# The last expert's second product in seven half-size products, in an attention and mixture-of-experts kernel

## The chip, the cores and the metric

The kernel runs on one core of a Trainium2 chip. The metric is the device time of one execution in microseconds (us). TensorE (PE in the profile) does the matrix products, VectorE (DVE) and ScalarE (ACT) the elementwise work, GpSimd (POOL) issues the gathers and scatters of token rows, SyncE (SP) issues the other transfers.

## The reference

An attention over a window of keys and over block summaries gives 3072 rows of 512 numbers. They go through a mixture of 8 experts, of which each row uses two:

```
logits = x @ w_gate;  noisy = logits + log1p(exp(x @ w_noise)) * noise
top2 = the two largest of noisy;  top2_w = softmax over these two
for e in range(8):
    for k in range(2):
        mask = top2[:, k] == e
        h = maximum(x[mask] @ w1[e], 0)              # 512 -> 1024
        out[mask] += top2_w[mask, k, None] * (h @ w2[e])   # 1024 -> 512
```

All data are 32-bit floats.

## The kernel before

After the attention the experts run one after the other, with room for 768 to 832 tokens each. Every 32-bit operand is split into two 16-bit floats, a high part and a rest (hi and lo), and every product is done in three passes: hi by hi, hi by lo, lo by hi. A split costs one copy on ACT (hi) and one subtraction on DVE (lo).

From the third expert on, the first product (x by w1) is done in seven products of half-size blocks instead of eight. The function `seven(e, i, u)` does product u = 1 to 7 for quarter i of the hidden features: `prod` issues its matmuls (L1365), and the sums that the scheme wants are built up in PSUM, with a copy on ACT (L1386, L1389) and an addition on DVE (L1391, L1393). The four blocks of hidden activations leave through a relu on ACT to `HT[0]` (hi, L1397) and a subtraction on DVE to `HT[1]` (lo, L1400).

The second product (h by w2) is plain: `mm2_part` issues for each chunk of 128 tokens 24 matmuls of 512 columns (8 row blocks of w2, three passes, L1437) into a PSUM buffer `pt`; `mm2_out` multiplies the chunk by the gate weight and adds the row that an earlier expert left (DVE, L932), and `y_scatter` writes it to `out` (POOL, L90). The earlier rows come by `prev_gather` (POOL, L90). The last expert (e = 7) has 768 tokens: six chunks.

The order of the work on each engine is the order in which the program is written. What is done for the next expert, or ahead of a use, is hung into that order by a table: `on(t, f, ...)` puts a call at step t, and `hook(t)` issues what stands there. A step of expert e thus holds loads (`w_load`, SP, L736), splits (`w_hi` on ACT, L741; `w_lo` on DVE, L759) and gathers. Four staging buffers (`stage`) take the loads. `og` is one PSUM tile of two banks, `b2` and `b5` are lists of two banks each, and `G["b1", i]` is `og[:, 0]` or a `pt` buffer in turn.

Of the kernel before, what the change touches and what calls it, by code (L numbers as in the profile page):

```python
# [8 lines left out]
F32 = mybir.dt.float32  # L9
# [4 lines left out]
AF = mybir.ActivationFunctionType  # L14
OP = mybir.AluOpType
# [5 lines left out]
P = 128  # L21
# [3 lines left out]
DM = H * D  # L25
E, F = 8, 1024
# [10 lines left out]
H0 = 384  # L37
# [7 lines left out]
SW = 16 * (D + 1)  # L45
# [5 lines left out]
GN = 4  # L51
WS = 16384.0
GROUP0 = 3
XS, W1S, W2S = 128.0, 32.0, 1024.0
# [9 lines left out]
def attn_moe(ctx, tc, qt, kt, vt, wgn, noise, w1, w2, out):  # L64
    nc = tc.nc
# [4 lines left out]
    psum = ctx.enter_context(tc.tile_pool(name="psum", bufs=1, space=PSUM))  # L70
# [4 lines left out]
    stage = ctx.enter_context(tc.tile_pool(name="stage", bufs=4))  # L75
# [3 lines left out]
    work = ctx.enter_context(tc.tile_pool(name="work", bufs=2, side="right"))  # L79
# [134 lines left out]
    late = []  # L214
# [212 lines left out]
    G = {}  # L427
# [290 lines left out]
    WT = {}  # L718
# [5 lines left out]
    SG, EV = {}, {}  # L724

    def w_load(e, i):
        s = stage.tile([P, SW], F32, name="stg")[:, :1024]
        SG[e, i] = s
        if i == 0:
            EV[e] = nc.values_load(eid[0:1, e:e + 1], engines=[mybir.EngineType.SP], min_val=0, max_val=E - 1) if e else 0  # L730
        if i < 4:
            nc.sync.dma_start(s, w1.rearrange("e d f -> (e d) f")[bass.ds(EV[e] * DM + i * P, P)])
        else:
            i -= 4
            rows = bass.ds(EV[e] * F + 2 * i * P, 2 * P)
            nc.sync.dma_start(s.rearrange("p (c d) -> p c d", c=2),  # L736
                              w2.rearrange("e f d -> (e f) d")[rows].rearrange("(c p) d -> p c d", p=P))
# [46 lines left out]
    def tb_of(e, c):  # L784
        return TB0[:, c] if e == 0 and c < 3 else TB[:, e, c]
# [85 lines left out]
    ow = {}  # L871
    pi_ = [0]

    def prev_gather(e, c):
        n = min(P, CAPS[e] - c * P)
        pv = PREV[pi_[0] % len(PREV)]
        pi_[0] += 1
# [12 lines left out]
        ow.setdefault(e, []).append(g)  # L890
        return pv
# [483 lines left out]
    def seven(e, i, u):  # L1375
        h = CAPS[e] // 2
        if u == 1:
            G["b1", i] = psum.tile([P, 512], F32, name="pt", bufs=2) if i % 2 else og[:, 0]
        b1, b2, b5 = G["b1", i][:, :h], G["b2"][i % 2][:, :h], G["b5"][i % 2][:, :h]
        hh, hl = HT  # L1380
        f = i + (4 if u in (4, 7) else 0)
        t = slice(0, h) if u in (2, 4) else slice(h + tail(e), 2 * h + tail(e))
        a, b = ((0, 0), (1, 1), (6, 2), (2, 6), (3, 3), (4, 5), (5, 4))[u - 1]
        prod(e, i, a, b, {1: b1, 2: b1, 3: b5, 5: b5}.get(u, b2), u in (1, 5))
        if u == 1:
            nc.scalar.activation(b2, b1, AF.Copy)  # L1386
# [12 lines left out]
        def lo():  # L1399
            nc.vector.scalar_tensor_tensor(hl[:, f, t], src, 0.0, hh[:, f, t], op0=OP.max, op1=OP.subtract)  # L1400

        return hi, lo

    def seven_head(e):
        if e == 2:
# [88 lines left out]
    for e in range(1, E):  # L1494
# [7 lines left out]
        if e == 1:  # L1502
# [9 lines left out]
        else:  # L1512
# [13 lines left out]
            if e > 2:  # L1526
                on(4, w_load, e, 6)
                on(4, w_load, e, 7)
        if n + 1 < E:
            on(40 if e == 1 else 43, xs_gather, n + 1, 0)  # L1530
            on(42 if e == 1 else 47, xs_gather, n + 1, 1)
        if n < E:
            on(44, w_load, n, 4)
            on(44, w_load, n, 5)
        if e == 1:
            on(48, w_load, n, 6)
            on(48, w_load, n, 7)
        for t in (17, 20, 23):
            on(t, prev)
        if e == 1:  # L1540
            for half in range(2):
                for f in range(FC):
# [169 lines left out]
```

## Time and profile before

| | us |
|---|---|
| median of 3 runs | 642.95 (642.61 to 643.33) |
| the profiled execution, as timed | 644.06 |
| its span in the trace | 642.2 |
| PE busy | 621.3 (97%), 5295 matmuls |
| DVE busy | 481.8 (75%) |
| ACT busy | 316.2 (49%) |
| POOL busy | 249.3 (39%) |

The trace comes from one execution. Busy time is the sum of an engine's instructions in the span. In tables of stretches a row holds the stretch and its length, then the busy time and, in brackets, the number of instructions of PE, PEld (PE's weight loads, which run beside the matmuls), DVE, ACT and POOL in this order, then the granted clock of TensorE as a share of full speed, the share of the DMA engines, and GB/s. In rows of single instructions the columns are the start, the time, the engine, the line, the operation, its output and inputs, and in square brackets how long the engine had been idle and what released it. An instruction's own time overlaps the next one's; the distance of two starts is what one costs in a row of them.

### The profile page before, as it was taken

How to read it: one execution, taken by the hardware profiler on the slowest of the kernel's cores; microseconds unless marked ns; L12 is line 12 of the kernel's file. 1: busy time of each engine (PE TensorE's matmuls, PEld its weight loads, DVE VectorE, ACT ScalarE, POOL GpSimd, SP SyncE). 2: the span in 40 equal slices, each digit the busy share in tenths (PEclk: the TensorE clock that was granted, in tenths of full speed). 3: DMA queues.
4: the chain of work that ended last, by engine and by line, in shares of the span. 5: the costliest groups of instructions: out<-in, count | busy, mean ns of one | idle time of the engine just before them, and what ended most of it. 6: DMA issues, size and time to landing. Idle time of an engine off the chain costs nothing. (4 is left out here: it accounts for less than half of the span.)

```text
span 642.2 us, 14122 instructions
## 1 busy us (share of the span) xinstructions
PE 621.3 (97%) x5295; PEld 360.3 (56%) x5295; DVE 481.8 (75%) x1039; ACT 316.2 (49%) x692; POOL 249.3 (39%) x432
## 2 busy tenths in 40 slices
PE   8899998899999999999999999999999999999995
PEld 7778787765554544555455544554554455445542
DVE  5858999789797598188868887987888679757510
ACT  4958988851163453075437534653464255425300
POOL 4443234203254434532573266336523532333041
PEclk9999999999999999999999999999999999999999
DMA  9999979778369786647986597769786768773021
GB/s 304 321 252 299 282 244 322 233 280 275 130 213 174 209 211 175 224 120 143 204 265 158 130 226 245 176 130 244 216 188 154 218 198 166 177 200 111 2 96 50
DMA packets 123707, 127.91 MB, mean 199 GB/s; under 512 B 83242, under 2 KB 86674, under 8 KB 123630
## 3 DMA queue, kind: packets, MB, share of 16 engines
q1 hardware_dynamic: 111838, 90.66, 53.6%
q0 software_dynamic: 11792, 36.27, 18.3%
q8 instruction: 43, 0.70, 0.5%
q14 instruction: 34, 0.28, 0.1%
HBM read 81.85 MB, written 25.61 MB: 167 GB/s over the span
## 5 line engine op out<-in xcount | busy, mean ns | idle before, releaser
L90 POOL DMA_INDIRECT out_dram<-y,tb x52 | 69.4, 1335 | 168.0 <-DVE y L932 129.6
L90 POOL DMA_INDIRECT xg<-xd,tb x54 | 60.4, 1119 | 119.8 <-DVE rh L1393 31.6
L1437 PEld LDWEIGHTS <-hth 128*128 128x128 f16 x576 | 56.4, 98 | 66.6
L932 DVE SCALAR_TENSOR_TENSOR y<-pt,tb,prev 128x512 f32<-128x512 f32 x42 | 31.5, 749 | 66.1 <-PE pt L1437 48.8
L1365 PEld LDWEIGHTS <-w1h 128*128 128x128 f16 x504 | 48.8, 98 | 38.8 <-issue 5.1
L1437 PE MATMUL pt<-w2h,htl 128*128 128x512 f16 x288 | 69.0, 379 | 0.0
L1437 PE MATMUL pt<-w2l,hth 128*128 128x512 f16 x288 | 69.0, 379 | 0.0
L1437 PE MATMUL pt<-w2h,hth 128*128 128x512 f16 x288 | 69.0, 379 | 0.0
L1365 PEld LDWEIGHTS <-w1l 128*128 128x128 f16 x504 | 49.3, 98 | 34.9
L90 POOL DMA_INDIRECT prev<-out_dram,tb x45 | 52.1, 1159 | 23.8 <-issue 13.4
L333 ACT ACTIVATE p<-s,nm 128x120 f32<-128x120 f32 x192 | 50.8, 376 | 0.8
L855 PE MATMUL h<-xte,w1h 128*128 128x384 f16 (+2 forms) x248 | 48.9, 336 | 0.0
L1437 PEld LDWEIGHTS <-htl 128*128 128x128 f16 x288 | 28.2, 98 | 34.0
L1354 ACT ACTIVATE w1h<-stg 128x768 f16<-128x768 f32 (+1 forms) x24 | 22.7, 944 | 40.4 <-DVE stg L1345 40.4
L1397 ACT ACTIVATE hth<-h 128x384 f16<-128x384 f32 (+4 forms) x48 | 23.8, 496 | 35.6 <-PE h L1365 34.1
L1365 PE MATMUL h<-xte,w1h 128*128 128x384 f16 (+4 forms) x180 | 39.7, 329 | 1.5 <-DVE h L1391 1.2
L1354 ACT ACTIVATE w1l<-stg 128x768 f16<-128x768 f32 (+1 forms) x24 | 22.5, 942 | 37.3 <-DVE stg L1345 37.3
L1365 PE MATMUL h<-xte,w1l 128*128 128x384 f16 (+4 forms) x180 | 39.7, 329 | 0.0
L1318 ACT ACTIVATE x<-xt 128x512 f16<-128x512 f32 (+2 forms) x44 | 26.5, 626 | 23.4 <-issue 20.1
L1345 DVE TENSOR_TENSOR stg<-stg 128x256 f32<-128x256 f32 x96 | 36.2, 418 | 0.8
L855 PEld LDWEIGHTS <-w1h 128*128 128x128 f16 x256 | 24.7, 98 | 19.4 <-issue 1.0
L1400 DVE SCALAR_TENSOR_TENSOR htl<-h,hth 128x384 f16<-128x384 f32 (+4 forms) x48 | 26.3, 562 | 11.8 <-ACT hth L1397 11.5
(310 smaller groups left out, 1296.7 us busy)
## 6 DMA issues: line engine op xcount, KB each, us to landing
stg<-in_w_dram SPq DMA_DIRECT2D x64, 512.0 KB
q<-in_qt_dram SPq DMA_DIRECT2D x24, 256.0 KB
out_dram<-xg SPq DMA_DIRECT2D x8, 768.0 KB
kb<-in_kt_dram SPq DMA_DIRECT2D x6, 768.0 KB
hth<-in_vt_dram SPq DMA_DIRECT2D x12, 260.0 KB
htl<-in_vt_dram SPq DMA_DIRECT2D x16, 195.0 KB
ve<-in_vt_dram SPq DMA_DIRECT2D x12, 260.0 KB
xd<-x SPq DMA_DIRECT2D x10, 256.0 KB
```

Source lines behind the costliest of these rows:

```text
L90: return nc.gpsimd.indirect_dma_start(**kw)
L333: nc.scalar.activation(PE_[t][:, a, hp, :], SC[t][:, a, hp, :], AF.Exp, bias=NM[t][:, 1, a, hp:hp + 1], scale=0.125)
L855: nc.tensor.matmul(ph[:, :n], w1_of(w, wn, c, f), x[:, xo + c, c0:c1], start=(k == 0), stop=(k == 11))
L932: nc.vector.scalar_tensor_tensor(y, py[:, :d], gw, pv[:, :d], op0=OP.mult, op1=OP.add)
L1318: nc.scalar.activation(t[:r, c:c + k], src, AF.Copy)
L1345: nc.vector.tensor_tensor(o, x, y, op=op)
L1354: nc.scalar.activation(hi, x, AF.Copy, scale=W1S)
L1365: nc.tensor.matmul(ph[:, :h], w[:, la, a, P * j:P * j + P], x[:, j, :h], start=start and k == 0, stop=k == 5, skip_group_check=True)
L1397: nc.scalar.activation(hh[:, f, t], src, AF.Relu)
L1400: nc.vector.scalar_tensor_tensor(hl[:, f, t], src, 0.0, hh[:, f, t], op0=OP.max, op1=OP.subtract)
L1437: nc.tensor.matmul(py, x, wv[:, f, :], start=st, stop=sp, skip_group_check=True)
```

## The change

Only the last expert (e = 7) is changed.

The second product is written as seven products of half-size blocks. The hidden activations are four blocks A11, A12, A21, A22 (384 tokens by 512 features), w2 is four blocks B11 to B22 (512 by 256). Four sums of activation blocks are made on DVE (`z_sums`), on the 32-bit values as they leave PSUM, and need A11 and A22 once more as 32-bit copies on ACT (`plus`). Four differences of weight blocks are made on DVE (`z_weight`). All sums are then split into hi and lo (`z_split`, `z_wsplit`). Each product has three chunks of 128 tokens with 12 matmuls of 256 columns, so 252 matmuls of 256 columns stand for 144 of 512. What the products share is built up in PSUM: A11·B11 is copied once (L1546), A1·B1 is copied to SBUF (`q5`, L1612) and added there (L1621). The output leaves in 18 steps of 128x256 on DVE (`put`, L1589) in place of six of 128x512.

Four more things move. The w2 of expert 7 is loaded during expert 6 into its token buffers (`G["zs"]`, the buffers of hi and lo tokens) instead of `stage`. All six gathers of earlier rows stand at steps 14 to 24 of expert 7. The chunks of a product stand in the order 0, 2, 1, with groups of PSUM banks p1, p2, p4, p5. The scatters stand at the end. The `else` below `plain` in the diff is the branch for the end of the last quarter, and the last block of the diff is in the table of steps of expert 6.

```diff
     def w_load(e, i):
-        s = stage.tile([P, SW], F32, name="stg")[:, :1024]
+        if "zs" in G and i >= 4:
+            s = G["zs"][i - 4]
+        else:
+            s = stage.tile([P, SW], F32, name="stg")[:, :1024]
...
     def seven(e, i, u):
...
+        if e == E - 1 and u in (2, 7, 3, 4):
+            return z_sums(i, u, src, hi, lo)
...
+    def z_sums(i, u, src, hi, lo):
...
+        def plus(name):
+            ZS[name, i] = work.tile([P, DM], F32, name="x", bufs=5)[:, :H0]
+            nc.scalar.activation(ZS[name, i], src, AF.Relu)
+        def hi_():
+            if u != 3:
+                hi()
+            if u in (2, 7):
+                plus({2: "a11", 7: "a22"}[u])
+        def lo_():
+            if u != 3:
+                lo()
+            if u == 3:
+                nc.vector.scalar_tensor_tensor(part(1), src, 0.0, ZS["a22", i], op0=OP.max, op1=OP.add)
+                nc.vector.scalar_tensor_tensor(part(3), src, 0.0, ZS["a11", i], op0=OP.max, op1=OP.subtract)
+                nc.vector.tensor_tensor(part(2), ZS[1, i], ZS["a11", i], op=OP.subtract)
+            elif u == 4:
+                nc.vector.scalar_tensor_tensor(part(4), src, 0.0, ZS[2, i], op0=OP.max, op1=OP.subtract)
...
+    def z_prod(a, b, ps, c, start, fs=range(4)):
+        za, zb = G["za"][a], G["zb"][b]
+        for la, lb in ((0, 0), (0, 1), (1, 0)):
+            for f in fs:
+                nc.tensor.matmul(ps[c], za[la][:, f, c * P:c * P + P], zb[lb][:, f], start=start, stop=True,
+                                 skip_group_check=True)
+                start = False
...
+    def last_expert(e):
...
+        order = (0, 2, 1)
+        p1 = [og[:, c // 2, HD * (c % 2):HD * (c % 2) + HD] for c in range(3)]
+        p2 = [x[:, :HD] for x in (b2[0], b5[1], b5[0])]
+        p5 = [x[:, :HD] for x in (og[:, 0], b2[1], og[:, 1])]
+        def plain(c):
+            z_prod("a11", "b11", p1, c, c != 1)
+            nc.scalar.activation(p2[c], p1[c], AF.Copy)
...
+            else:
+                plain(0)
+                h7[1]()
+                plain(2)
+                for j in range(2):
+                    z_wsplit(j, 1, 1)
+            h3 = seven(e, i - 1, 3)
...
+            if i == 4:
+                plain(1)
+            h4 = seven(e, i - 1, 4)
...
+        def put(c, half, ps):
+            y = ZP[c][:, HD * half:HD * half + HD]
+            nc.vector.scalar_tensor_tensor(y, ps, gws[c], y, op0=OP.mult, op1=OP.add)
+        for fs in (range(3), range(3, 4)):
+            for c in order:
+                z_prod("a12", "b21", p1, c, False, fs)
...
+        for c in order:
+            z_prod("a22", 4, p4, c, c != 1)
+        for c in order:
+            put(c, 0, p1[c])
...
+        for c in order:
+            z_prod(1, 1, p5, c, True)
+            nc.scalar.activation(q5[:, c], p5[c], AF.Copy)
...
+        for c in order:
+            z_prod(2, 2, p2, c, False)
+            nc.vector.tensor_tensor(p5[c], p2[c], q5[:, c], op=OP.add)
+        for c in order:
+            put(c + 3, 1, q5[:, c])
+        for j in (1, 2, 3):
+            z_split(4, j, 1)
+        for c in order:
+            z_prod(3, 3, p2, c, False)
+            put(c + 3, 0, p2[c])
+            put(c + 3, 1, p2[c])
+            y_scatter(e, c + 3, ZP[c + 3])
+        for c in order:
+            z_prod(4, "b22", p5, c, False)
+            put(c, 1, p5[c])
+            y_scatter(e, c, ZP[c])
...
+            if n == E - 1:
+                on(37, z_init)
+                for t, i in ((38, 4), (39, 6), (41, 5), (42, 7)):
+                    on(t, w_load, n, i)
+                for j in range(2):
+                    on(45 + j, z_weight, j, 3)
+                    on(45 + j, z_weight, j, 1)
-        if n < E:
+        if n < E - 1:
             on(44, w_load, n, 4)
             on(44, w_load, n, 5)
```

The kernel after is longer than the one before, so its lines have other numbers: L1391, L1393, L1397 and L1400 of before are L1395, L1397, L1401 and L1404 of after.

On VectorE the first place is the end of the first product of expert 7, from the addition of product 6 in the last quarter to the split of the block A22 (`h`, `rh` and `pt` are PSUM banks or the buffer of the block A22). Before:

```order
L1391 TENSOR_TENSOR h<-h,p_7895 128x384
L1400 SCALAR_TENSOR_TENSOR htl<-pt,hth 128x384
L1400 SCALAR_TENSOR_TENSOR htl<-h,hth 128x384 x2
L1393 TENSOR_TENSOR rh<-h,p_7895 128x384
L1400 SCALAR_TENSOR_TENSOR htl<-rh_3813,hth 128x384
```

On VectorE, the same place now:

```order
L1395 TENSOR_TENSOR h<-h,p_7930 128x384
L1404 SCALAR_TENSOR_TENSOR htl<-pt,hth 128x384
L1439 SCALAR_TENSOR_TENSOR xt<-h,x 128x384
L1440 SCALAR_TENSOR_TENSOR xt<-h,x 128x384
L1441 TENSOR_TENSOR xt<-xt,x 128x384
L1404 SCALAR_TENSOR_TENSOR htl<-h,hth 128x384
L1443 SCALAR_TENSOR_TENSOR xt<-h,xt 128x384
L1498 SCALAR_TENSOR_TENSOR w1l_320<-xl,w1h_319 128x1024
L1397 TENSOR_TENSOR rh_3813<-h,p_7930 128x384
L1404 SCALAR_TENSOR_TENSOR htl<-rh_3813,hth 128x384
```

Between the first addition and the one that makes `rh` there were three instructions; now there are seven: four more sums, one split less of a hidden block, and a split of 1024 weight columns.

On ScalarE, at the same place, now:

```order
L1401 ACTIVATE hth<-pt 128x384
L1427 ACTIVATE x<-pt 128x384
L1500 ACTIVATE w1h_319<-xg_165 128x512
L1500 ACTIVATE w1h_319<-xg_166 128x512
L1401 ACTIVATE hth<-h 128x384
L1401 ACTIVATE hth<-rh_3813 128x384
L1427 ACTIVATE x<-rh_3813 128x384
L1546 ACTIVATE h<-o 128x256 x3
L1401 ACTIVATE hth<-h 128x384
```

The three copies of A11·B11 (L1546) stand behind the relu and the 32-bit copy of the block that VectorE's `rh` addition makes. Before, only relus stood here.

The second place is the end of the program on VectorE, from the additions of `q5` on. Before, its last rows were six like this one, each behind a chunk of 24 matmuls, and a scatter on POOL behind each:

```order
L1400 SCALAR_TENSOR_TENSOR htl<-rh_3813,hth 128x384
L1400 SCALAR_TENSOR_TENSOR htl<-h,hth 128x384 x2
L932 SCALAR_TENSOR_TENSOR y<-pt,tb,prev_2952 128x512
L932 SCALAR_TENSOR_TENSOR y<-pt,tb,prev_2950 128x512
L932 SCALAR_TENSOR_TENSOR y<-pt,tb,prev_2951 128x512
```

On VectorE, the end now:

```order
L1621 TENSOR_TENSOR o<-h,stg 128x256 x2
L1621 TENSOR_TENSOR h<-h,stg 128x256
L1589 SCALAR_TENSOR_TENSOR y<-stg,tb,y 128x256 x3
L1472 TENSOR_TENSOR w1l_2943<-stg,w1l_2943 128x768
L1472 TENSOR_TENSOR w1l_2943<-xt,w1l_2943 128x384
L1472 TENSOR_TENSOR w1l_2943<-w1l_320,w1l_2943 128x384
L1589 SCALAR_TENSOR_TENSOR y<-h,tb,y 128x256 x6
L1589 SCALAR_TENSOR_TENSOR prev_2952<-o,tb,prev_2952 128x256
L1589 SCALAR_TENSOR_TENSOR prev_2951<-o,tb,prev_2951 128x256
L1589 SCALAR_TENSOR_TENSOR prev_2950<-h,tb,prev_2950 128x256
```

Fifteen puts and splits now lie between the last addition and the end. On POOL six scatters follow the sixfold puts without a gather between them; the six gathers stand a product earlier.

On SyncE the third place is the last part of expert 6. Before, the loads of expert 7's w2 stood behind all token transposes of expert 7 and went to `stage`:

```order
L1334 DMA_TRANSPOSE w2h_2944<-x 128x6x128
L1334 DMA_TRANSPOSE w2l_2945<-x 128x8x128
L1334 DMA_TRANSPOSE xte<-x 128x6x128
L1334 DMA_TRANSPOSE xte<-x 128x8x128
L736 ISA
L736 DMA stg<-in_w_dram 128x2x512
```

On SyncE, the same place now:

```order
L739 ISA
L739 DMA xte<-in_w_dram 128x2x512
L1338 DMA_TRANSPOSE w2h_2944<-x 128x6x128
L1338 DMA_TRANSPOSE w2l_2945<-x 128x8x128
L739 ISA
L739 DMA xte<-in_w_dram 128x2x512
L1338 DMA_TRANSPOSE xte<-x 128x6x128
L1338 DMA_TRANSPOSE xte<-x 128x8x128
```

Two of the four loads now stand between and ahead of these transposes, and their target is the buffer that held expert 6's tokens.

## Rows read from the trace of the kernel before

**Rows 1.** Table by stretch: first product, then second product, of the last expert

```profile
580.00:600.00 20.00, 20.00 (x125) 12.05 (x124) 14.40 (x23) 11.28 (x21) 5.29 (x8) 1.00 0.27 79
600.00:620.00 20.00, 20.00 (x100) 9.68 (x99) 5.36 (x10) 2.48 (x5) 4.40 (x8) 1.00 0.17 54
```

**Rows 2.** Chain of waits, its end (start, time, engine, what)

```profile
605.39 29.58 PE pt L1437 x137
...
635.00 0.76 DVE y L932
```

**Rows 3.** Instructions of PE, second product

```profile
614.08 1.89 PE L1437 MATMUL pt<-w2h,hth 128*128 128x512 f16 x8
...
619.26 1.89 PE L1437 MATMUL pt<-w2h,hth 128*128 128x512 f16 x8
```

**Rows 4.** Instructions of PE, first product, third quarter

```profile
588.12 0.81 PE L1365 MATMUL h<-w2l,w1h 128*128 128x384 f16 x4
...
589.10 0.81 PE L1365 MATMUL h<-w2l,w1l 128*128 128x384 f16 x4
```

**Rows 5.** Instructions of VectorE, first quarter into second

```profile
580.84 0.55 DVE L1391 TENSOR_TENSOR h<-h,p 128x384 f32<-128x384 f32 x1
581.30 2.35 DVE L759 SCALAR_TENSOR_TENSOR w2l<-stg,w2h 128x1024 f16<-128x1024 f32 x2
583.57 0.55 DVE L1393 TENSOR_TENSOR rh<-h,p 128x384 f32<-128x384 f32 x1
```

**Rows 6.** Instructions of ScalarE, same stretch

```profile
579.93 1.99 ACT L741 ACTIVATE w2h<-stg 128x1024 f16<-128x1024 f32 x2
...
584.15 0.52 ACT L1397 ACTIVATE hth<-rh 128x384 f16<-128x384 f32 x1 [0.25 <-DVE rh L1393]
584.58 0.47 ACT L1397 ACTIVATE hth<-pt 128x384 f16<-128x384 f32 x1
```

**Rows 7.** Groups by line and shape, whole span (busy us, mean ns)

```profile
L932 DVE SCALAR_TENSOR_TENSOR y<-pt,tb,prev 128x512 f32<-128x512 f32 x42 | 31.5, 749 | 66.1 <-PE pt L1437 48.8 <-issue 9.8 <-PE pt L910 7.4
L1328 DVE TENSOR_TENSOR x<-xt,x 128x512 f16<-128x512 f32 x36 | 23.6, 684 | 0.0
L1328 DVE TENSOR_TENSOR x<-xg,x 128x256 f16<-128x256 f32 x18 | 7.5, 417 | 0.0
L1318 ACT ACTIVATE x<-xg 128x256 f16<-128x256 f32 x18 | 7.3, 406 | 0.1
```

**Rows 8.** Instructions of POOL, gathers and the first and last scatter of expert 7

```profile
587.52 1.01 POOL L90 DMA_INDIRECT prev<-out_dram,tb  x1 [0.22 <-issue]
...
588.84 1.59 POOL L90 DMA_INDIRECT prev<-out_dram,tb  x1 [0.21 <-issue]
...
610.14 1.00 POOL L90 DMA_INDIRECT out_dram<-y,tb  x1 [19.61 <-DVE y L932]
...
636.03 0.97 POOL L90 DMA_INDIRECT out_dram<-y,tb  x1 [4.11 <-DVE y L932]
```

**Rows 9.** Instructions of PE behind its pauses (idle time in brackets)

```profile
31.80 0.37 PE L354 MATMUL o<-htl,pts 120*64 120x65 f32 x1 [1.76 <-DMA htl<-in_vt_dram]
...
523.54 0.65 PE L1365 MATMUL h<-xte,w1h 128*128 128x384 f16 x3 [1.01 <-DVE h L1391]
```

**Rows 10.** Table by stretch around these two pauses, columns as in rows 1

```profile
30.00:32.00 2.00, 0.24 (x5) 0.20 (x6) 2.00 (x4) 1.97 (x8) 0.38 (x2) 0.88 1.04 353
32.00:34.00 2.00, 2.00 (x32) 1.88 (x31) 0.91 (x3) 0.77 (x4) 1.16 (x3) 0.50 1.08 261
34.00:36.00 2.00, 2.00 (x41) 1.49 (x41) 0.89 (x2) 0.60 (x1) 0.00 (x0) 0.77 1.01 335
522.00:524.00 2.00, 0.99 (x7) 0.48 (x5) 1.97 (x4) 1.84 (x4) 0.97 (x2) 1.00 0.02 4
```

**Rows 11.** Loads of expert 7's w2 on SyncE's queue

```profile
565.91 14.95 SPq L736 DMA_DIRECT2D stg<-in_w_dram  x4
```

**Rows 12.** Instruction of VectorE in expert 6, with the idle time before it

```profile
571.44 0.75 DVE L932 SCALAR_TENSOR_TENSOR y<-pt,tb,prev 128x512 f32<-128x512 f32 x1 [3.30 <-PE pt L1437]
```

More of the change, by code (lines that the diff above doesn't have):

```diff
@@ L872, in attn_moe, with prev_gather @@
     pi_ = [0]
-    def prev_gather(e, c):
+    def prev_gather(e, c, pv=None):
         n = min(P, CAPS[e] - c * P)
-        pv = PREV[pi_[0] % len(PREV)]
-        pi_[0] += 1
+        if pv is None:
+            pv = PREV[pi_[0] % len(PREV)]
+            pi_[0] += 1
         if c == LAST and not four(e, c):
@@ L1400, in lo, with part @@
             nc.vector.scalar_tensor_tensor(hl[:, f, t], src, 0.0, hh[:, f, t], op0=OP.max, op1=OP.subtract)
+        if e == E - 1 and u in (2, 7, 3, 4):
+            return z_sums(i, u, src, hi, lo)
         return hi, lo
+    ZS = {}
+    def z_sums(i, u, src, hi, lo):
+        def part(k):
+            if i < 2:
+                ZS[k, i] = G["zt"][k - 1][:, H0 * i:H0 * i + H0]
+            elif i == 2:
+                ZS[k, i] = work.tile([P, DM], F32, name="xt", bufs=GN)[:, :H0]
+            elif k < 3:
+                ZS[k, i] = XP2[k - 1].rearrange("p s c -> p (s c)").bitcast(F32)[:, DM:DM + H0]
+            else:
+                x = WT[0][("w1h", "w1l")[k - 3]].rearrange("p a b -> p (a b)").bitcast(F32)
+                ZS[k, i] = x[:, 1536:1536 + H0]
+            return ZS[k, i]
+        def plus(name):
[15 more added lines that the diff above has]
+                nc.vector.scalar_tensor_tensor(part(4), src, 0.0, ZS[2, i], op0=OP.max, op1=OP.subtract)
+        return hi_, lo_
@@ new lines, in z_split, with z_stage, z_temp @@
+    def z_split(k, j, low):
+        a, b = G["za"][k]
+        if j < 2:
+            x, hi, lo = G["zt"][k - 1][:, :2 * H0].rearrange("p (f c) -> p f c", f=2), a[:, 0:2], b[:, 0:2]
+        else:
+            x, hi, lo = ZS[k, j], a[:, j], b[:, j]
+        if low:
+            nc.vector.tensor_tensor(lo, x, hi, op=OP.subtract)
+        else:
+            nc.scalar.activation(hi, x, AF.Copy)
+    def z_stage(i):
+        return SG[E - 1, i].rearrange("p (c d) -> p c d", c=2)
+    def z_temp(j):
+        return XP2[j].rearrange("p s c -> p (s c)").bitcast(F32)[:, :DM].rearrange("p (c d) -> p c d", c=2)
@@ new lines, in z_weight, with z_wsplit @@
+    def z_weight(j, k):
+        s, t = z_stage(4 + j), z_stage(6 + j)
+        d = {3: z_temp(j), 1: s[:, :, HD:], 2: t[:, :, HD:], 4: t[:, :, :HD]}
+        a, b = {3: (s[:, :, HD:], t[:, :, HD:]), 1: (s[:, :, HD:], s[:, :, :HD]), 2: (t[:, :, HD:], s[:, :, HD:]),
+                4: (t[:, :, :HD], t[:, :, HD:])}[k]
+        nc.vector.tensor_tensor(d[k], a, b, op=OP.subtract)
+    def z_wsplit(j, k, low):
+        if k == 3:
+            x = z_temp(j)
+        elif k in ("b2", 42):
+            x = z_stage(6 + j)
+        else:
+            x = z_stage(4 + j)[:, :, HD if k == 1 else 0:][:, :, :HD]
+        hi, lo = [y[:, 2 * j:2 * j + 2] for y in G["zb"][k]]
+        if low:
+            nc.vector.scalar_tensor_tensor(lo, x, W2S, hi, op0=OP.mult, op1=OP.subtract)
+        else:
+            nc.scalar.activation(hi, x, AF.Copy, scale=W2S)
@@ L1511, in attn_moe @@
             plan_w1(n, 3, 13, 38, 38, 39, 39, 39)
-        else:
+        elif n < E:
             for i, (a, b) in enumerate(((3, 4), (4, 7), (8, 14), (15, 21))):
@@ L1528, in attn_moe @@
                 on(4, w_load, e, 7)
+            if n == E - 1:
+                on(37, z_init)
+                for t, i in ((38, 4), (39, 6), (41, 5), (42, 7)):
+                    on(t, w_load, n, i)
+                for j in range(2):
+                    on(45 + j, z_weight, j, 3)
+                    on(45 + j, z_weight, j, 1)
         if n + 1 < E:
@@ L1537, in attn_moe @@
             on(48, w_load, n, 7)
-        for t in (17, 20, 23):
+        for t in (17, 20, 23) if n < E else ():
             on(t, prev)
+        if e == E - 1:
+            last_expert(e)
+            break
         if e == 1:
```

87 lines of the change are left out of this document (added), and 3 rows, old and new, of the table c.

## The prediction, made before the changed kernel ran

> **What bounds the kernel now.** I read the chain of waits first. From 605.39 it is one run of PE matmuls, 29.58 us, then one DVE instruction, then a scatter [rows 2]. So in the second product of the last expert PE alone decides, and the tail is one DVE step and one scatter. The tables by stretch say the same for the 20 us before: PE is busy in all 20.00 us of 580 to 600 and of 600 to 620 [rows 1], so DVE and ACT, though busy, are in time. What differs is the slack. DVE has 14.40 of 20 us to do in the first product and 5.36 in the second [rows 1]. The change takes matmul time out of the second and puts DVE and ACT work into both, a good part of it into the first, at the place where both products meet. The question is whether DVE and ACT stay in time.
>
> **The matmuls: −3.5.** Twenty-four matmuls of 512 columns start at 614.08 and the next at 619.26 [rows 3], .2158 each; 144 of them are 31.1 us. Matmuls of 256 columns are not in the trace. Six of 384 took .98 (588.12 to 589.10) [rows 4], .163 each. The step from 384 to 512 columns is .0525 for 128, so 256 should take .163 − .053 = .110, and 252 of them 27.6. The bounds are .108 (half of a 512, 27.2 us) and .163 (no faster than 384, 41.1). Weight loads were 9.68 us for 99 [rows 1], .098 each beside the matmuls, under .110, so I take .110.
>
> **Wait in the third quarter: +1.05.** DVE's steps in a row cost their distance: 384 columns .47 (580.84 to 581.30, where .55 is its own time), 1024 columns 1.13 (two from 581.30 to 583.57) [rows 5]. ACT's are .43 for 384 (584.15 to 584.58) and .95 for 1024, or 1.05 alone [rows 6]. At the place of rows 5, DVE's addition for the block A22 ends at 583.57 + .55; ACT's relu starts at 584.15. ACT now does the relu .43, the 32-bit copy .43 and a weight split 1.05: 586.06 before it reaches the next block's relu. DVE's split of that weight part (1.13) and then, at .47 each, the addition of product 6, the split of the next block and the first new sum, and .56 for the second, which reads the PSUM bank that product 5 of the next quarter writes: 586.06 + 1.13 + 3 x .47 + .56 = 589.16. PE wants that bank at 588.12 [rows 4]: 1.05 us late. None of this is hidden, since PE does nothing else meanwhile. Bounds 0 and 2.
>
> **Wait before product 7 of the last quarter: +.4.** ACT has a split of 768 columns (two of 384, about .83) between DVE's addition for A22 and the relu on it, and DVE has a split, a weight split (1.13) and the addition of product 6 (.55) behind that. By the same steps product 7 is .4 late. Bounds 0 and 1.
>
> **Where the products meet: +3.4.** Let T be the start of DVE's addition of product 6 in the last quarter. DVE has seven steps of 384 columns, 7 x .47 = 3.29, a weight split of 1.13, and then the addition for A22, .55: T + 4.97. Then ACT does the relu on it (.43) and its 32-bit copy (.43), and only then the copy of A11·B11's first chunk, .40 (406 ns for 256 columns [rows 7]) and .04 on the way: T + 6.27. The second chunk's first matmul waits for that copy, since both chunks lie in the one PSUM tile `og`. PE at that time is through with product 7 and the first chunk: .55 + .98 + 12 x .110 = 2.85. It waits 3.4 us. Behind that matmul on PE stand all that is left; nothing else is ready for it. Before, the matmuls of the plain product stood here and needed only hidden blocks done long ago. Bounds: .55, if the copy is not held up (its own .40 and two handovers), and 4.2, with each step at its own time and not at its distance.
>
> **Two waits in the second product: +.55 and +1.1.** Product A1·B1 writes its chunks to `og`, other `og` bank, other chunk: the second waits for ACT's copy of the first, .40 and some .15 of handovers; bounds 0 and 1. In the last product the second chunk is to write the same tile after DVE's `put` of the first. Count from the end of the last matmul of the product before the last but one. DVE: .04, an addition .40, three puts of `q5` at .40, splits of 768 and 384 and 384 columns (.87 + .47 + .47), six puts at .40 and one of .48. (For 256 columns: 417 ns for an addition, 684 for 512; the put's 749 for 512 [rows 7] makes 749 − 267 = 482; in a row .08 less.) That is 6.33. PE: 36 + 12 matmuls, 5.25. So 1.1; bounds 0 (puts as fast as additions without the splits in the way) and 3.8 (puts of .75 each).
>
> **The tail: +1.2.** Scatters now follow one another. In a row POOL's indirect transfers are 1.32 apart (587.52 to 588.84) [rows 8]. From the same zero the first is issued at .04 + .40 + 1.20 + 1.81 + .40 + .48 + .27 = 4.60, the .27 being what lay between the last DVE step and the scatter before (635.76 to 636.03) [rows 2, 8]. The sixth then starts at 4.60 + 5 x 1.32 = 11.20. PE's end is 5.25 + 1.08 + 24 x .110 = 8.97. So the last scatter starts 2.23 after PE, where before it was 1.06 (634.97 to 636.03) [rows 2, 8]. Bounds −.3 (POOL keeps up) and 3 (each as long as the 1.59 of the third gather [rows 8], and more between).
>
> **The sum of waits:** −3.5 + 1.05 + .4 + 3.4 + .55 + 1.1 + 1.2 = +4.2.
>
> **The clock: +1.6.** After PE had stood for 1.76 us until 31.80 [rows 9], the granted clock was .88, .50 and .77 in the three stretches from 30 to 36 [rows 10]: the lower level, 1.2 GHz, for .2 + 2.0 + .9 us after PE went on. Matmuls at half the clock lose half of that, 1.55 us. A pause of 1.01 us before 523.54 [rows 9] left the clock at 1.00 [rows 10]. The waits of 1.05, .4, .55 and 1.1 are like the second; the 3.4 is longer than the first. I take it that the clock falls once, for 1.55, about 1.6; bounds 0 and 3.2 (twice).
> The Trainium skill, page "TensorE: Matmul & The Clock Gate", section "HAM oscillation — how this bites in real kernels", says that a pause of PE between two bursts of matmuls brings the lower clock back, so that the next burst starts at it. By that rule 648.7 comes out, and without it 647.1; the trace agrees in the one pause and not in the other.
>
> **Costed at nothing.** The eight weight differences of 512 columns in expert 6, .68 each, go into DVE's idle time there (3.30 us before 571.44 alone [rows 12]). The six early gathers, 6 x 1.32 = 8 us, fall into POOL's idle 19.61 us before 610.14 [rows 8]. The loads of w2 carry the same bytes as before. They took 14.95 us from 565.91, because each waited for a staging buffer [rows 11]; now they wait for expert 6's tokens, which are read by then. On SyncE two of them stand ahead of transposes for expert 7; if their target came free late, the transposes behind would be late too. That is the cover that could be gone (third rival).
>
> **Rivals.**
> 1. The waits come, the clock stays: 642.95 + 4.2 = 647.1. For it: only one pause in the trace shows a fall, and there PE had been busy in short pieces. Against it: 3.4 is twice that pause.
> 2. DVE and ACT keep up; the place is the meeting of the products. If their steps cost a third less than my distances, the first two waits vanish, the 6.27 becomes 4.2 and the wait 1.35, in the second product .4 and 0 stay (6.33 becomes 4.2, under PE's 5.25), and the tail, set by POOL's 1.32, is .75: 2.5 in all. With matmuls at their lower bound, −3.9, and no fall of the clock, that is −1.4, 641.5, faster. It decides from a distance of about .38 for 384 columns, a fifth less, where the waits are 3.5 and eat up the gain; rows 5 have .47. Against it: the steps of 384 columns in rows 5 are of the kind that is added. For it: additions between two SBUF tiles, and ACT's copies between them, are not all shown.
> 3. The loads come late. If the last of the four lands at 580.86 as before [rows 11], DVE stands in front of the weight differences, and behind them the sums for expert 7's first product, which PE needs. About 3.3 us more: 652.0. For it: the loads' target is a buffer that another expert has just used. Against it: they are issued earlier and no longer wait for staging.
> 4. Half of the waits: the chunks of `og` don't wait for one another, so 3.4 becomes about 2, the .55 and 1.1 go, no fall of the clock: −3.5 + 1.05 + .4 + 2 + 1.2 = +1.1, 644.1.
>
> **How the numbers follow.** The profiled execution took 644.06, its span 642.2 and 1.86 around it, 1.11 above the median of 642.95. The sum is made against it: 644.06 + 5.8 = 649.9 there; the same step from the median gives 648.7, and the rivals are counted from the median too. Chances: forecast .53 (own range 647.4 to 650.4), rival 1 .20, rival 2 .12, rival 3 .07, rival 4 .08. A measurement of this kernel tells from no change what is over .2%, 1.3 us. Faster by more than that (under 641.7): most of rival 2, .09. Within it (to 644.2): the rest of rival 2 and half of rival 4, .07. Slower: .84. The range from 644.3 to 651.3 leaves out rival 2, half of rival 4 and rival 3's upper part, .2 in all.
>
> **What would show it.** Right: in the profile after, PE idle for 3 to 4 us where the products meet, released by ACT's copy L1546, with DVE and ACT without a gap there; pauses of about 1 us in the third quarter (released by DVE L1440) and in the last product (released by DVE L1589); a granted clock of about .5 for 2 to 4 us behind the long pause; matmuls of 256 columns .110 apart; the last scatter 2.2 us after PE's end. Wrong: PE in one run through the second product, or matmuls of 256 columns well above .110, or PE idle before product 1 of expert 7, with DVE waiting for a load in expert 6.

## The result, and the profile after

The changed kernel took 651.52 us (median of 4 runs, 648.87 to 652.24), the kernel before 643.14 beside it: ratio 1.012, 95% interval 1.0088 to 1.0153. Medians and ratios here and below leave out a few executions in a slower state, and a ratio with its interval is estimated on its own, so it is not exactly the quotient of the two medians (1.013 here). By the medians the kernel is slower by 8.4 us, by the ratio by 7.7, where 5.8 were forecast; 651.52 is just above the range of 644.3 to 651.3, and 1.012 times the 642.95 from which the forecast counted is 650.7, inside it. The profiled execution took 651.93, its span is 650.1, against 644.06 and 642.2 before.

PE's idle times in the last expert come first. These are the instructions of PE behind its pauses, all of them from 579 on (the idle time and its releaser are in the brackets):

```profile
590.08 0.81 PE L1369 MATMUL h<-w2l,w1h 128*128 128x384 f16 x4 [1.08 <-DVE stg L1440]
...
603.32 0.81 PE L1369 MATMUL h<-w2l,w1l 128*128 128x384 f16 x4 [0.40 <-DVE h L1395]
...
608.99 0.60 PE L1506 MATMUL o<-w2h,hth 128*128 128x256 f16 x4 [3.23 <-ACT h L1546]
...
625.09 0.60 PE L1506 MATMUL o<-w2h,hth 128*128 128x256 f16 x4 [0.52 <-ACT stg L1612]
...
638.12 0.60 PE L1506 MATMUL o<-w2h,w1l 128*128 128x256 f16 x4 [1.08 <-DVE prev L1589]
```

Five pauses, in the five places of the forecast and with the releasers it named: 1.08 (1.05 forecast), 0.40 (0.4), 3.23 (3.4), 0.52 (0.55) and 1.08 (1.1). Before, PE ran through here in one piece [rows 1, 2]. The table by stretch (columns as in rows 1), first 20 us each, then 2 us each behind the long pause:

```profile
580.00:600.00 20.00, 18.92 (x117) 11.24 (x115) 17.36 (x31) 13.38 (x27) 9.13 (x14) 1.00 0.31 90
600.00:620.00 20.00, 16.38 (x117) 11.91 (x115) 13.32 (x24) 11.11 (x24) 0.00 (x0) 0.91 0.00 1
...
608.00:610.00 2.00, 1.01 (x9) 0.87 (x9) 1.71 (x3) 0.94 (x3) 0.00 (x0) 0.98 0.03 8
610.00:612.00 2.00, 2.00 (x10) 1.13 (x8) 0.06 (x1) 0.37 (x1) 0.00 (x0) 0.50 0.00 0
612.00:614.00 2.00, 2.00 (x13) 1.40 (x12) 1.11 (x3) 0.00 (x0) 0.00 (x0) 0.67 0.00 0
```

DVE has 17.36 of 20 us to do where it had 14.40 [rows 1], and behind the pause the granted clock is at 0.50, the lower of its two levels. What the long pause is made of stands in the instructions of DVE, and then ACT, before it:

```profile
602.71 0.56 DVE L1395 TENSOR_TENSOR h<-h,p 128x384 f32<-128x384 f32 x1
603.22 0.56 DVE L1404 SCALAR_TENSOR_TENSOR htl<-pt,hth 128x384 f16<-128x384 f32 x1
603.69 0.55 DVE L1439 SCALAR_TENSOR_TENSOR xt<-h,x 128x384 f32<-128x384 f32 x1
604.15 0.55 DVE L1440 SCALAR_TENSOR_TENSOR xt<-h,x 128x384 f32<-128x384 f32 x1
604.62 0.55 DVE L1441 TENSOR_TENSOR xt<-xt,x 128x384 f32<-128x384 f32 x1
605.08 0.56 DVE L1404 SCALAR_TENSOR_TENSOR htl<-h,hth 128x384 f16<-128x384 f32 x1
605.55 0.55 DVE L1443 SCALAR_TENSOR_TENSOR xt<-h,xt 128x384 f32<-128x384 f32 x1
606.01 1.22 DVE L1498 SCALAR_TENSOR_TENSOR w1l<-xl,w1h 128x1024 f16<-128x1024 f32 x1
607.15 0.56 DVE L1397 TENSOR_TENSOR rh<-h,p 128x384 f32<-128x384 f32 x1
```

```profile
607.74 0.52 ACT L1401 ACTIVATE hth<-rh 128x384 f16<-128x384 f32 x1 [3.13 <-DVE rh L1397]
608.17 0.51 ACT L1427 ACTIVATE x<-rh 128x384 f32<-128x384 f32 x1
608.58 0.36 ACT L1546 ACTIVATE h<-o 128x256 f32<-128x256 f32 x1
```

DVE has no idle time from its first addition (602.71) to the one that makes the block A22 (607.15). ACT stands idle for 3.13 us waiting for that block, and only then copies the chunk of A11·B11 that PE had finished at 605.8. A busy engine (DVE) holds an idle one (ACT), and that holds PE.

The balance, from the start of expert 7's second product of blocks (PE's first matmul behind expert 6) to the end. That stretch begins at 578.37 before and 579.08 after. Its first matmuls before, then its first and last matmuls and the last scatter after:

```profile
578.37 0.81 PE L1365 MATMUL o<-w2h,w1h 128*128 128x384 f16 x4
```

```profile
579.08 0.81 PE L1369 MATMUL o<-w2h,w1h 128*128 128x384 f16 x4
...
640.30 0.60 PE L1506 MATMUL h<-w2h,w1l 128*128 128x256 f16 x4
...
642.84 0.98 POOL L90 DMA_INDIRECT out_dram<-prev,tb  x1 [0.24 <-issue]
```

| | before | after | difference |
|---|---|---|---|
| start of the stretch | 578.37 | 579.08 | +0.7 |
| from there to PE's end | 56.6 | 61.8 | +5.2 |
| from PE's end to the start of the last scatter | 1.06 | 1.94 | +0.9 |
| from there to the end of the span | 6.2 | 7.3 | +1.1 |

The +5.2 are -3.6 of columns, +7.1 of waits and +1.7 of clock. The columns: 48 matmuls of 256 columns from 626.39 to 631.63 are .109 each, 27.5 us against 31.1. The waits: the five idle times sum to 6.3; counted by starts they are 7.1, because a matmul's time in a row overlaps the next one's by some .16, and a pause takes that overlap away (the group before the long one started at 605.17 and held four at .11; the next could have started at 605.61, and started at 608.99). The clock: six matmuls of 384 columns from 610.65 took 1.92 instead of .98 [rows 4], two groups of four of 256 columns .79 and .81 instead of .44:

```profile
609.86 1.00 PE L1506 MATMUL o<-w2h,htl 128*128 128x256 f16 x4
610.65 1.49 PE L1369 MATMUL h<-w2h,w1l 128*128 128x384 f16 x4
611.93 0.85 PE L1369 MATMUL h<-xte,w1l 128*128 128x384 f16 x2
612.57 0.98 PE L1506 MATMUL o<-w2h,hth 128*128 128x256 f16 x4
613.38 0.60 PE L1506 MATMUL o<-w2l,hth 128*128 128x256 f16 x4
...
626.39 0.60 PE L1506 MATMUL h<-w2h,hth 128*128 128x256 f16 x4
...
631.63 0.60 PE L1506 MATMUL h<-w1h,w1h 128*128 128x256 f16 x4
```

### The profile page after: what moved, and what is told of

It is laid out like the page before. It is cut to its first block, busy times and chain, and to the rows that moved or that the text cites. A ratio compares the mean times of both kernels' runs of the same rounds, so it can differ in the third digit from the quotient of the medians.

```text
span 650.1 us, 14419 instructions
## 1 busy us (share of the span) xinstructions
PE 621.3 (96%) x5403; PEld 372.3 (57%) x5403; DVE 506.2 (78%) x1092; ACT 328.8 (51%) x720; POOL 250.5 (39%) x432
## 4 chain that ended last, share of the span: by engine, by line
PE 73%; DVE 10%; DMA 6%; ACT 5%; issue 2%; SPq 2%; POOL 1%; POOLq 0%; DVEq 0%; ACTq 0%
PE pt L1670 23%; PE h L1369 13%; PE h L858 10%; PE pt L914 7%; PE h L914 2%; PE pt L1369 2%; PE o L1369 2%; DMA q<-in_qt_dram 2%; ACT p L333 2%; DMA kb<-in_kt_dram 2%; PE o L354 2%; DVE htl L1404 2%; PE o L1506 2%; DMA htl<-in_vt_dram 2%; PE pt L341 1%
## 5 line engine op out<-in xcount | busy, mean ns | idle before, releaser
L90 POOL DMA_INDIRECT out_dram<-y,tb x49 | 66.8, 1362 | 176.4 <-DVE y L936 92.1
L90 POOL DMA_INDIRECT xg<-xd,tb x54 | 60.6, 1122 | 119.9 <-DVE dsc L654 32.5
L1670 PEld LDWEIGHTS <-hth 128*128 128x128 f16 x480 | 47.0, 98 | 55.5
L90 POOL DMA_INDIRECT prev<-out_dram,tb x42 | 49.8, 1185 | 20.7 <-issue 12.3
L1670 PE MATMUL pt<-w2l,hth 128*128 128x512 f16 x240 | 57.5, 379 | 0.0
L1670 PE MATMUL pt<-w2h,hth 128*128 128x512 f16 x240 | 57.5, 379 | 0.0
L1670 PE MATMUL pt<-w2h,htl 128*128 128x512 f16 x240 | 57.5, 379 | 0.0
L936 DVE SCALAR_TENSOR_TENSOR y<-pt,tb,prev 128x512 f32<-128x512 f32 x36 | 27.0, 749 | 38.2 <-PE pt L1670 21.1
L1670 PEld LDWEIGHTS <-htl 128*128 128x128 f16 x240 | 23.5, 98 | 28.3
L1401 ACT ACTIVATE hth<-h 128x384 f16<-128x384 f32 (+4 forms) x44 | 21.9, 498 | 28.9 <-PE h L1369 27.4
L325 DVE TENSOR_REDUCE nm<-s 128x8 f32<-128x960 f32 x24 | 27.7, 1154 | 5.8 <-PE s L318 4.7
```

The costliest lines, as they stand in the source:

```text
L90: return nc.gpsimd.indirect_dma_start(**kw)
L325: nc.vector.tensor_reduce(NM[t][:, 0], SC[t], axis=AX.X, op=OP.max)
L936: nc.vector.scalar_tensor_tensor(y, py[:, :d], gw, pv[:, :d], op0=OP.mult, op1=OP.add)
L1670: nc.tensor.matmul(py, x, wv[:, f, :], start=st, stop=sp, skip_group_check=True)
```

## The experiments

For each kernel its own profile gives the stretch from expert 7's second product of blocks to the start of the last scatter: 57.66 in the kernel before, 63.76 and 63.42 in two profiles of the changed one. That is a better measure of expert 7 than the whole time, since the start of this stretch lay between 577.0 and 581.2 in the kernels that follow, and the time from the last scatter to the end between 6.1 and 7.5, in no order that the edits explain.

| kernel | stretch | median time, ratio to the kernel before beside it (95% interval) |
|---|---|---|
| again | 63.4 | 650.86, 1.0098 (1.0059 to 1.0138) |
| copies_first | 60.6 | 648.38, 1.0061 (1.0037 to 1.0086) |
| filler | 62.1 | 650.80, 1.0110 (1.0072 to 1.0149) |
| banks_apart | 59.5 | 647.19, 1.0045 (1.0016 to 1.0075) |
| steps_moved | 59.7 | 648.12, 1.0042 (1.0020 to 1.0063) |
| splits_early | 63.5 | 652.93, 1.0096 (1.0062 to 1.0130) |
| copies_steps_early | 58.3 | 645.78, 1.0014 (0.9990 to 1.0037) |
| all | 57.2 | 645.37, 0.9999 (0.9977 to 1.0021) |
| copies_steps_banks | 57.2 | 644.17, 0.9996 (0.9969 to 1.0022) |
| all_trail | 55.5 | 642.87, 0.9978 (0.9947 to 1.0009) |
| early_trail | 62.1 | 649.15 (one run) |
| all_trail12 | 55.6 | 641.66, 0.9955 (0.9927 to 0.9984) |

**again**, the changed kernel without an edit.

> The changed kernel once more, to have its time on the chip on which the next three run. Every theory: about 651.5, some 8 us over the kernel before, with pauses of PE of about 1.1, 0.4, 3.2, 0.5 and 1.1 us at the same five places, and the granted clock near 0.5 behind the pause of 3.2. If the 1.1 us by which the end of the program (from the last scatter's start to the span's end) was longer than before, and the 0.7 us by which expert 7 started later, are chance, they differ here.

The five pauses came again (1.07, .39, 3.22, .52, 1.08). The start of expert 7 was 577.96 and the end 6.5 long, so the +0.7 and the +1.1 of the first profile are not fixed costs of the change. The clock fell to 0.50 again, here before PE went on: counted as above, that cost 1.35, and 1.7 in the first profile, which is nearly the whole difference of the two stretches.

**copies_first**

```diff
             h7 = seven(e, i - 1, 7)
+            if i == 4:
+                plain(0)
+                plain(2)
             h7[0]()
...
-                plain(0)
                 h7[1]()
-                plain(2)
```

> The first two chunks of A11 B11 and their ACT copies are issued ahead of the relu and the 32-bit copy of the last block A22. My theory: PE's pause where the products meet is ACT's copy standing behind DVE's queue, so it falls from 3.2 to about 0.5, no pause over 1 us takes its place, the clock stays at 1.00 there, and the time is 651.5 - 2.7 - 1.7 = 647.1. Rival: DVE and ACT have more to do there than PE leaves time for in any order, so the pause of about 3 us only moves to the next product that needs their blocks, and the time stays above 650.5.

PE behind its pauses where the products meet:

```profile
606.71 0.60 PE L1506 MATMUL o<-w2h,hth 128*128 128x256 f16 x4 [0.84 <-ACT h L1546]
...
612.25 0.49 PE L1506 MATMUL o<-w2h,hth 128*128 128x256 f16 x3 [0.81 <-ACT h L1546]
```

The 3.2 became .84, and the clock stayed at 1.00 (604 to 616). The forecast missed the second pause, .81, at the next product: there ACT's copy of the third chunk waits for a bank that DVE's late sums still read (its releaser is DVE L1440). So the rival had a quarter of it right: DVE's work moves a part of the wait on. The stretch is 2.8 to 3.1 shorter, 4.4 were expected.

**filler**

```diff
                 plain(0)
+                idle = psum.tile([P, 512], F32, name="pt", bufs=2)[:, :HD]
+                for k in range(2):
+                    z_prod("a11", "b11", [idle], 0, True)
                 h7[1]()
```

> 24 more matmuls of 256 columns (2.6 us) into a spare PSUM bank, of which nothing is read, stand where PE waits 3.2 us. ACT's copy comes when it came. If the pause itself brings the lower clock: pause about 0.7, granted clock 1.00 from there on, 651.5 - 1.7 = 649.8. If the clock falls for another reason, or the slow matmuls behind the pause have another cause: the same slow stretch, 651.5 or a little more.

PE's pause, and the clock in the two stretches of 2 us behind it:

```profile
609.05 0.60 PE L1506 MATMUL o<-w2h,hth 128*128 128x256 f16 x4 [0.60 <-ACT h L1546]
```

```profile
608.00:610.00 2.00, 1.40 (x14) 1.11 (x12) 1.66 (x3) 0.99 (x3) 0.00 (x0) 1.00 0.00 0
610.00:612.00 2.00, 2.00 (x18) 1.50 (x17) 0.51 (x2) 0.37 (x1) 0.00 (x0) 1.00 0.00 0
```

ACT's copy comes no earlier, PE only does useless work meanwhile, and the clock stays at 1.00. The stretch is 1.4 to 1.7 shorter: that is the price of the lower clock, shown alone. The whole time (650.80) can't be told from that of the changed kernel; the profile can.

**banks_apart**

```diff
-        p1 = [og[:, c // 2, HD * (c % 2):HD * (c % 2) + HD] for c in range(3)]
+        p1 = [og[:, 0, :HD], og[:, 0, HD:], None]
-        p5 = [x[:, :HD] for x in (og[:, 0], b2[1], og[:, 1])]
+        p5 = [og[:, 0, :HD], b2[1][:, :HD], None]
...
+                p1[2] = p5[2] = psum.tile([P, 512], F32, name="pt", bufs=2)[:, :HD]
...
-        pts = [psum.tile([P, 512], F32, name="pt", bufs=2) for i in range(2)]
-        p4 = [pts[c // 2][:, HD * (c % 2):HD * (c % 2) + HD] for c in range(3)]
+        pts = psum.tile([P, 512], F32, name="pt", bufs=2)
+        p4 = [pts[:, :HD], pts[:, HD:], og[:, 1, :HD]]
```

> The third chunk of A11 B11 and of A1 B1 gets a PSUM tile of its own instead of the second bank of og; the third chunk of the product A22 by the fourth weight sum takes that bank. My theory: the waits are those of one tile. The second chunk (in time) starts without a pause; the next chunk, still in og, waits about 1.3 for ACT's copy; the pauses of 0.5 and 1.1 in the second product go; the clock stays at 1.00. 2.1 + 1.7 + 0.7 = 4.4 less, 647.1; the last pause gives nothing, since the scatters follow one another at 1.3 us and set the end. Rival (DVE and ACT have too much to do in any order): over 650.

One pause is left where the products meet, at the chunk that stays in `og`, and none in the second product:

```profile
609.88 0.60 PE L1506 MATMUL o<-w2h,hth 128*128 128x256 f16 x4 [0.94 <-ACT h L1546]
```

So the waits are those of one tile that several chunks share: in the changed kernel the first and the second chunk in time lie in different banks of `og`, and PE waited all the same. That ACT's order makes the long one long is what copies_first showed. The stretch is 3.9 to 4.2 shorter, 4.4 were expected. PE's end comes 5.1 to 5.5 earlier; the last scatter doesn't follow all of it, since the scatters now set the end, as expected.

**steps_moved**

```diff
-                             (5, "b2", 0, 0), (8, "b2", 0, 1), (9, "b2", 1, 0), (10, "b2", 1, 1),
-                             (12, 1, 0, 0), (13, 1, 1, 0), (18, 42, 0, 0), (23, 42, 1, 0), (24, 42, 0, 1),
-                             (25, 3, 0, 0), (26, 3, 1, 0), (28, 42, 1, 1)):
+                             (5, "b2", 0, 0), (8, "b2", 0, 1), (11, "b2", 1, 0), (13, "b2", 1, 1),
+                             (12, 1, 0, 0), (13, 1, 1, 0), (18, 42, 0, 0), (23, 42, 1, 0),
+                             (25, 3, 0, 0), (26, 3, 1, 0)):
-        for t, k in ((21, 1), (22, 2)):
+        for t, k in ((20, 1), (20, 2)):
...
-                for j in range(2):
-                    z_wsplit(j, 1, 1)
...
+        for k in (42, 1):
+            for j in range(2):
+                z_wsplit(j, k, 1)
```

> Only weight splits and two splits of activation sums are issued at other places: one pair two and three steps later in the second quarter, two ACT splits of 768 columns one and two steps earlier, and the rests of 3 weight blocks on VectorE only behind the last block of the first product. My theory: the pauses of 1.1 and 0.4 in the first product are these splits standing ahead of what PE waits for, so both go; the pause where the products meet loses one split of 1.13 and is 2.1, long enough that the clock still falls. From the start of expert 7's product 2 to the start of the last scatter it took 63.8 and 63.4 in the two profiles of the changed kernel: 63.6 - 1.25 - 0.55 - 1.1 = 60.7 here; in all 2.9 less. Rival: DVE and ACT are short of time in any order, so the pauses come back at the next use: 63 or more.

The pauses of 1.08 and .40 are gone. One of .39 came before product 5 of the last quarter, where PE waits for a sum that DVE makes from the second quarter, and one of .23 behind the meeting (617.00). The first of these, and the meeting:

```profile
594.13 0.81 PE L1369 MATMUL h<-w2l,w1l 128*128 128x384 f16 x4 [0.39 <-DVE stg L1440]
...
604.18 0.60 PE L1506 MATMUL o<-w2h,hth 128*128 128x256 f16 x4 [1.74 <-ACT h L1546]
```

The 2 us that hold its pause and the 2 us behind them:

```profile
602.00:604.00 2.00, 0.44 (x5) 0.24 (x3) 1.41 (x3) 1.08 (x3) 0.00 (x0) 1.00 0.00 0
604.00:606.00 2.00, 1.82 (x16) 1.48 (x16) 0.04 (x1) 0.44 (x2) 0.00 (x0) 1.00 0.03 8
```

The pause fell to 1.74 (2.1 expected) and the clock held, which I had not expected; so, in spite of the two new pauses, the stretch is 59.7 and not 60.7.

**splits_early**

```diff
+        for j in (1, 2, 3):
+            z_split(4, j, 1)
         for c in order:
             z_prod(2, 2, p2, c, False)
...
-        for j in (1, 2, 3):
-            z_split(4, j, 1)
         for c in order:
             z_prod(3, 3, p2, c, False)
```

> The three low splits of the fourth activation sum stand ahead of the additions of q5 instead of ahead of the last puts. My theory: they fill 2.7 us in which DVE waits for PE, the first scatter comes 1.8 us earlier, the pause of 1.1 in the last product falls to 0.5, and the last scatter starts 1.5 earlier (62.1 from product 2). Rival: the end is set by something else than DVE's queue (POOL's 1.3 us per scatter beginning where it begins), 63.5.

A miss: 63.5. The first scatter did come 1.8 earlier and the pause in the last product did fall, to .57, but at the very end something new stands, in PE's last matmuls, DVE's last put and the last scatter:

```profile
641.54 0.60 PE L1506 MATMUL h<-w2h,w1l 128*128 128x256 f16 x4
...
643.61 0.48 DVE L1589 SCALAR_TENSOR_TENSOR prev<-h,tb,prev 128x256 f32<-128x256 f32 x1 [2.26 <-PE h L1506]
...
644.38 0.97 POOL L90 DMA_INDIRECT out_dram<-prev,tb  x1 [1.71 <-DVE prev L1589]
```

The trace puts the wait of this put down to PE, whose last matmul ends at 642.14, but the put starts 1.5 us later. In the changed kernel the same put starts at once (640.94, PE's end at 640.90).

**copies_steps_early** and **all**: the edits of copies_first, steps_moved and splits_early together, in the second that of banks_apart too.

> Copies first, steps moved and splits early together, with the banks of the changed kernel. If the terms add: from product 2 to the last scatter 53.1 of matmuls without a pause, 0.7 and 0.6 of pauses in the second product, about 1.0 where the products meet, 1.1 tail = 56.5, where the kernel before had 57.7: about 1 us under the kernel before. If DVE and ACT are short of time: 59 or more, not under before.

> The same three and the banks apart. If the terms add, no pause over 0.3 us is left in expert 7: 53.1 of matmuls and 1.1 to 1.5 of tail = 54.4, 3.3 under the kernel before, ratio 0.995, with the clock at 1.00. If DVE and ACT are short of time in any order: 58 or more, no faster than before.

The matmul side added up in `all`: from 580.11 PE ends at 634.37, 54.3 with two pauses of .39 and .23. But the last put came at 636.50, 2.1 us after PE, and took back 1.6: 57.2, level with the kernel before, where 54.4 were expected. Copies_steps_early had a lateness of 1.5 (58.3, where 56.5 were expected). In `all` the trace names no engine of the kernel as what released the put (`remote`):

```profile
633.77 0.60 PE L1506 MATMUL h<-w2h,w1l 128*128 128x256 f16 x4
...
636.50 0.48 DVE L1592 SCALAR_TENSOR_TENSOR prev<-h,tb,prev 128x256 f32<-128x256 f32 x1 [2.44 <-remote]
```

**all_trail, early_trail, copies_steps_banks**

```diff
             y_scatter(e, c, ZP[c])
+        for k in range(2):
+            z_prod("a11", "b11", [b2[0][:, :HD]], 0, True)
```

> The kernel with copies first, steps moved, splits early and banks apart, and 24 more matmuls of 256 columns (2.6 us) behind the last product, into a bank whose values are used no more. In the three kernels with the splits early, the last put on DVE started 1.5 to 2.1 us after PE's last matmul, with a load of PE's program code in the DMA queues at that moment; in the others 0.0 to 0.3. Theory: PE's report of its last matmul is held up by what PE's sequencer does at the end of the program (the branch and the code behind it, fetched while the scatters fill the queues). With other matmuls behind the last one its report is prompt, the last scatter starts 1.3 after the fifth: 55.6 from product 2 of expert 7 (57.2 without the trail, 57.7 in the kernel before), 1.6 us less than without the trail. Rival: the report is late for another reason (the scatters' own traffic): 57.2, no gain.

> The changed kernel with the splits early alone, and the same 24 matmuls at the end. Theory: what splits_early missed (62.1 expected, 63.5 measured) was the late report, so 62.1 comes now. Rival: 63.5 again.

> Copies first, steps moved, banks apart, the low splits of the fourth sum where the changed kernel has them. If the terms add: no pause over 0.4 in expert 7; the first scatter comes some 1.5 later than with the splits early, and six of them at 1.28 set the end: 56.9 from product 2, 0.8 under the kernel before. Rival: late report of the last matmul here too: no loss, since the sixth scatter waits for POOL.

The diff is the trail, 24 matmuls at the end of the program. All_trail is `all` with it, early_trail is splits_early with it; copies_steps_banks is `all` with the low splits of the fourth sum where the changed kernel has them, and no trail. Both stretches with a trail came out as the theory said, 55.5 and 62.1, with the last put at once behind the last matmul that it needs. So the miss of splits_early was the late report of that matmul, and useless matmuls behind it make it prompt. That it was PE's sequencer and the code behind the branch is consistent with this, but not shown. The load of program code, of which the expectation speaks, is not enough by itself: a load of 16 KB on the same queue (q8) starts 0.1 to 0.5 us before PE's end in the late kernels, and 0.5 and 0.4 us before it in the changed kernel and in copies_steps_banks, whose last put is prompt (0.04 us behind PE). The part that the scatters' traffic plays was not tried apart. Copies_steps_banks came out at 57.2, where 56.9 were expected: PE's end is 54.0 from the start of the stretch, and the scatters set the end.

**all_trail12**, with `z_prod` once instead of twice.

> The best version, with 12 matmuls behind the last product instead of 24 (1.3 us instead of 2.6). The last scatter should start 55.5 after product 2 again, if 1.3 us are enough to let the last report go out promptly. From the last scatter's start to the span's end it was 7.3 with 24, where the kernel before had 6.2 and the other kernels 6.1 to 7.3. If PE's longer work at the end is what draws it out, it is 6.2 to 6.6 now and the time some 2 us under the kernel before (ratio 0.997); if that is chance, anything in that span, and the same ratio as with 24, 0.998. If 1.3 us are too short, the last put is late again and 57 comes.

PE behind its pauses in expert 7, DVE's last put and the last scatter:

```profile
598.31 0.81 PE L1369 MATMUL h<-w2l,w1l 128*128 128x384 f16 x4 [0.41 <-DVE stg L1440]
...
619.29 0.60 PE L1506 MATMUL o<-w2h,hth 128*128 128x256 f16 x4 [0.23 <-DVE prev L1592]
```

```profile
635.48 0.48 DVE L1592 SCALAR_TENSOR_TENSOR prev<-h,tb,prev 128x256 f32<-128x256 f32 x1 [0.83 <-PE h L1506]
```

```profile
636.72 0.97 POOL L90 DMA_INDIRECT out_dram<-prev,tb  x1 [0.24 <-issue]
```

Its stretch is 55.6, 2.1 under the kernel before, the end 6.1, and the time 641.66 beside 643.60: 1.9 us less by the medians (0.997), and 0.9955 (0.9927 to 0.9984) by the ratio. So it beats both kernels, the one before by a few tenths of a per cent. Whether the 24 matmuls of the longer trail draw the end out (7.3 and 7.5 there) is not decided, since kernels without a trail lie between 6.1 and 7.3. What bounds it at the end is POOL: six scatters at 1.29 us from 630.28 on.

## Why the prediction was right

- Matmuls: .110 forecast, .109 measured; -3.5 forecast, -3.6 measured.
- The wait in the third quarter, the one before product 7 and the two in the second product: 1.05, .4, .55 and 1.1 forecast, 1.08, .40, .52 and 1.08 measured as idle time. Each was worked out as a queue of steps at the distance of two starts, not at a step's own time; that is what made them fit. In the sum each was .15 to .2 too small. The last two were counted from the end of a matmul, which leaves out the overlap of matmuls that a pause takes away. The first was counted from a start, and by starts it measured 1.25; there the near agreement with 1.08 is in part luck, since DVE's queue came .2 later than worked out. Steps_moved shows the cause of the first two, banks_apart that of the last two; that these came at all answers the fourth rival, in which the chunks of `og` don't wait for one another.
- Where the products meet: 3.4 forecast, 3.23 measured, 3.4 by starts. Copies_first and banks_apart each take most of it away, from the two sides that the step named: ACT's order, and the one tile `og`.
- The clock: 1.6 forecast, 1.7 measured, and 1.4 to 1.7 by filler. It fell once, behind the long pause, so the first rival was wrong. The Trainium skill, page "TensorE: Matmul & The Clock Gate", section "HAM oscillation — how this bites in real kernels", says that a long enough wait between bursts of matmuls lets the next burst start at the lower clock. The traces agree in that a pause of 3.2 us brought 0.50, and the four of .40 to 1.08 did not; the next burst did start at it in `again`, but in the first profile it ran at 1.00 for .9 us and fell then.
- The tail: 1.2 forecast, .9 measured; the scatters followed one another at 1.29 and not 1.32, which is half of the difference, and PE's end came .13 later than counted, which is the rest.
- One sign failed: "DVE and ACT without a gap there". DVE had none; ACT stood idle for 3.13 us, as the forecast's own sum has it, in which ACT waits for DVE.
- Costed at nothing: from one and the same first-product matmul of expert 4 to the start of expert 7 it was 177.5 before (400.89 to 578.37), 177.3 after (401.75 to 579.08) and 177.4 in again. The weight differences, the loads and the gathers cost nothing there. Not all eight differences stand in expert 6, as the prediction has it: four do (568.77 to 574.83), and four stand in expert 7's first product (591.34 to 598.14), where none of the changed kernel's pauses is released by them. The third rival was near: DVE waited for the last load once, without holding up anyone.

```profile
574.10 0.69 DVE L1487 TENSOR_TENSOR xg<-xte,xl 128x512 f32<-128x512 f32 x1 [1.20 <-DMA xl<-in_w_dram]
```

- What the sum lacks: it gives +5.8, the profile's stretch to the last scatter +6.1, and the medians +8.4. The +5.8 and the +6.1 are close in part by luck: the waits were .6 too small, the tail .3 too large. Between +6.1 and +8.4 lie the first 580 us and the last 7, where the runs spread over more than a microsecond each way. In `again`, with more runs on both sides, the stretch is +5.8 and the medians differ by 6.3, so most of the 2.3 did not come again. Only one profile of the kernel before was taken, so it stays open whether a part of it is the change's.

One step was wrong beside the forecast, in the second rival: it let DVE and ACT keep up only with faster steps (under .38 for 384 columns). In all_trail12 the steps stand at the same distance (.47), and the same instructions on DVE and ACT, in another order and with chunks in other banks, leave PE .6 us of pauses. The work fits; its order and its banks did not.

## What to carry to other kernels

When matmul time is cut, write down for each block what the slower engines do between its end and its next use, in the order of their queues and at the distance of starts, and put the copy that PE waits for ahead of the block that DVE delivers late. Chunks that share one tile wait for one another's readers: give the chunk that comes next another tile. A pause of PE behind which the clock falls costs more than its length: 3.2 us cost 1.3 to 1.7 more here.

## What the runs showed of the hardware

- A pause of 1.74 us (steps_moved) left the granted clock at 1.00; one of 1.76 us before 31.80 in the kernel before [rows 9, 10] brought the lower level. PE had been busy in all of the 4 us up to 602 ahead of the first, and in 3.94 of the 4 us up to 30 ahead of the second. Every pause of 3.2 us (four profiles) brought the lower level. So the length of a pause does not tell by itself for lengths between.
- PE's last matmul of the program was reported 1.5 to 2.1 us late in the three kernels with the splits early and no matmuls behind it, at once in those with 12 or 24 behind it, and 0.04 to 0.3 us behind PE's end in the kernels with the splits late. The cause is open.
